# Recording only the second of two exponentials as user of a PSUM group, where the group spans two pairs' buffers

## The chip, the cores and the metric

The kernel runs on one core of one Trainium2 chip. The time is device time in microseconds of one execution, and the median of several runs is given. A profile of one execution was taken with the hardware profiler; its span runs from the first instruction to the last.

## What is computed

Queries are averaged two by two, scored against all keys, passed through a softmax and applied to the values. The result, put back in token order, goes through a layer with a maximum of two projections and an output projection.

```python
q_pool = q.reshape(B, H, S // 2, 2, D).mean(axis=3)      # B 8, H 8, S 1152, D 64
scores = np.matmul(q_pool, k.transpose(0, 1, 3, 2)) / np.sqrt(D)
attn = softmax(scores)                                   # over the keys
x = np.matmul(attn, v).transpose(0, 2, 1, 3).reshape(B * S // 2, H * D)   # 4608 x 512
out = np.maximum(x @ w1, x @ w2) @ w_out                 # 512 -> 1024 -> 512
```

## The kernel before

The 64 heads are worked on as 32 pairs of heads. For a pair, POOL adds neighbouring queries (qp) and casts keys (kbf) and values (vE). The queries are transposed to qpT: by PE for the first five pairs, and from pair 5 on (`Q_PE = 5`) by eight 32-row transposes on DVE, `qtrans_dve` at L378, where the eighth (n = 7) alone is recorded as the writer of qpT. The keys are transposed to kT by PE for the first pairs and by a DMA later.

The scores of all pairs form one long row of columns, 5184 (`PW`) for each pair, and this row is cut into 324 groups of 512 columns (`W`). For a group, PE computes the scores of both heads into one of the PSUM tiles sps (L515), and ACT takes the exponential of both heads' 512 columns (L522, 128 x 1024 elements) into the SBUF tile et. Three sps tiles take turns at first; from the point `turn_at` on there are two, and the third serves other matmuls. et has room for two pairs (one of each parity), so its columns wrap after every second pair, that is every 10368 columns. Every fourth such wrap falls on a group's edge; at the other 12 the group is split, and ACT runs two exponentials, one up to `turn` and one from it. They are 256 and 768, 512 and 512, or 768 and 256 elements of a partition, in rotation.

When a pair's exponentials are done, PE multiplies them with the values (L425 and L437, called attention-times-V here) into a bank of fb or of the third sps tile, and DVE divides by the sums (L447 to L457). Blocks of the later layers fill PE in between: L727 makes the hidden values, DVE applies the ReLU (L736), L760 makes the output, DVE copies it out of PSUM (L771). When the scores are all done, the rest of these blocks follows (L700 and L793).

The order on each engine is not written by hand. A planner (`Plan`) records every operation with the keys that it reads and writes, and a scheduler picks PE's next unit by planned times. `deps` makes an operation depend on the last writer of each key that it reads or writes, and on the readers of each key that it writes; only the former, for keys that it reads, are kept as raw dependencies. `solve` turns dependencies into semaphore waits. A dependency on an operation of the same engine is left out by this line (L102), unless it is a raw one on an engine other than PE:

```python
if p["eng"] == eng and not o["fence"] and (eng == "PE" or eng != "DVE" and d not in o["raw"]):
    continue
```

A wait is also left out where the engine has already waited for a later operation of the same engine. Each exponential reads the key s{r} of its sps tile and writes it too, so that the next scores into that tile wait for it. Where a group is split, both halves do so.

Of the kernel before, what the change touches and what calls it, by code (L numbers as in the profile page):

```python
# [16 lines left out]
class Plan:  # L17
# [40 lines left out]
    def op(self, eng, fn, r=(), w=(), dma=None, cost=0.1, mode="f", after=(), solo=False,  # L58
           fence=False):
        n = len(self.ops)  # L60
        assert all(k in self.writer for k in r), r
        deps, raw = self.deps(r, w, after)
        prev = self.last.get(eng)
        if prev is not None and (solo or self.ops[prev]["solo"]):
            deps.add(prev)
            raw.add(prev)
        self.last[eng] = n
        t = self.when(eng, r, w, after, fence)
        if dma is not None:
            if not self.dma_free:  # L70
                t = 0.78
            self.free[eng] = t + (1.3 if mode == "t" else 0.5)
            a = max(self.free[eng] + 1.2, self.dma_free)
            self.dma_free = a + cost + (1.9 if a < 5.0 <= a + cost else 0.0)
            seen = self.dma_free + 0.7
        else:
            if eng == "PE" and mode != self.mode:
                t += 0.1
                self.mode = mode
            self.free[eng] = t + cost  # L80
            seen = t + cost + self.LAT[eng]
        self.ops.append(dict(eng=eng, fn=fn, deps=deps, raw=raw, dma=dma, w=tuple(w),
                             seen=seen, end=self.free[eng], solo=solo, fence=fence))
        for k in r:
            self.readers.setdefault(k, set()).add(n)
        for k in w:
            self.writer[k] = n
            self.readers[k] = set()
        return n
# [72 lines left out]
def bass_funnel_attn__then__act_maxout2_kernel(  # L162
# [32 lines left out]
    with ctx:  # L195
        def sbuf(shape, dt, name):
            return ctx.enter_context(nc.sbuf_tensor(name, list(shape), dt))
# [9 lines left out]
        qp = [t[0:HP, :, :, :] for t in qpw]  # L207
        qpf = [t.rearrange("p u h d -> p (u h d)")[:, 0:QU * D].rearrange("p (u d) -> p u d", d=D)
               for t in qpw]
        qpT = [sbuf([P, SQ], BF16, f"qpT{s}") for s in range(3)]  # L210
        kbf = [sbuf([P, NT, 2, D], BF16, f"kbf{s}") for s in range(2)]
        kT = [sbuf([P, NT, P], BF16, f"kT{s}") for s in range(3)]
# [27 lines left out]
        def rows(half):  # L240
            return slice(half * HP, half * HP + HP)

        Q0 = (0, 4, QU)
        QA = 4 * HP
# [127 lines left out]
        def qtrans_dve(i, n):  # L372
            s, z = i % 2, i % 3
            h, pb, db = n // 4, n // 2 % 2, n % 2
            src, dst = 64 * h + 32 * pb, 64 * h + 32 * db
            view = qpT[z][:, :].rearrange("p (u x) -> p u x", x=HP)
            last = [f"qpT{z}"] + (["qpT0.0"] if i == 3 else []) if n == 7 else []
            op("DVE", lambda e: e.transpose(  # L378
                view[dst:dst + 32, :, 32 * pb:32 * pb + 32],
                qpf[s][src:src + 32, :, 32 * db:32 * db + 32]),  # L380
                r=[f"qp{s}.0", f"qp{s}.1"], w=last, after=[f"qpT{z}"] + (["qpT0.0"] if i == 3 else []), cost=0.37)
            if n == 7:
                q_done.add(i)

# [81 lines left out]
        def first(i):  # L466

            return i * PW // W
# [15 lines left out]
        def pieces(g):  # L484

            a = g * W
            while a < (g + 1) * W:
                i = a // PW
                x = a - i * PW
                for c, z in runs(i):  # L490
                    if x < NT * (z - c):
                        break
                    x -= NT * (z - c)
                t, lo = x // (z - c), c + x % (z - c)
                n = min((g + 1) * W - a, z - lo)
                yield i, t, lo, lo + n, a - g * W
                a += n

        def pairs_of(g):
            return sorted({i for i, *_ in pieces(g)})  # L500

        def skeys(g):
            return [key for i, t, lo, *_ in pieces(g) for key in (
                f"kT{i % 3}.{t}", "qpT0.0" if i == 0 and lo < QA else f"qpT{i % 3}")]

        def ring(g):
            return g % 3 if g < turn_at[0] else (g - turn_at[0]) % 2

        def scores(g):
            r = ring(g)  # L510

            def pe(e):
                for i, t, lo, hi, col in pieces(g):
                    for h in range(2):
                        last = e.matmul(  # L515
                            sps[r][:, h, col:col + hi - lo], kT[i % 3][rows(h), t, :],
                            qpT[i % 3][rows(h), lo:hi], start=True, stop=True)
                return last

            def exp(a, z, keys):  # L520
                c = a % (2 * PW)
                op("ACT", lambda e: e.activation(  # L522
                    et2[:, :, c:c + z - a], sps[r][:, :, a - g * W:z - g * W], EXP, scale=scale),
                    r=[f"s{r}"], w=keys + [f"s{r}"], cost=0.05 + (z - a) / 600.0)

            op("PE", pe, r=skeys(g), w=[f"s{r}"], cost=PE_S, mode="s")
            a, z = g * W, (g + 1) * W
            turn = z // (2 * PW) * 2 * PW
            keys = {i: [f"et{i % 2}.{g - first(i)}"] for i in pairs_of(g)}
            if a < turn < z:  # L530
                i = turn // PW
                exp(a, turn, keys[i - 1])
                exp(turn, z, keys[i])
            else:
                exp(a, z, sum(keys.values(), []))
# [331 lines left out]
        Q_PE = 5  # L867
# [72 lines left out]
        def flush():  # L940
# [21 lines left out]
            if turns and plan.free.get("DVE", 0.0) <= now():  # L962
                qtrans_dve(*turns.pop(0))
# [75 lines left out]
        def banks(job, kk):  # L1039
            if job.single:  # L1040
                return [f"f{kk}", f"f{kk + 1}"]
            return [f"f{kk + (len(job.units[0]) > 4)}"]
# [23 lines left out]
        def burst_now(size):  # L1066

            todo_g = range(nxt, min(nxt + size, NGR))
            if not todo_g:
                return None, 0.0  # L1070
            for g in todo_g:
                for p, t, *_ in pieces(g):
                    if (any(key not in plan.writer for key in skeys(g)) if p == 0 else p not in q_done) or k_hi.get(p, 0) <= t or (
                            p >= 2 and av_half.get(p - 2) != 2):
                        return None, 0.0
            t = now() + 0.1
            stall = 0.0
            for g in todo_g:
                s = plan.when("PE", r=skeys(g), w=[f"s{ring(g)}"])
                stall += max(0.0, s - t)  # L1080
                t = max(t, s) + PE_S
            return todo_g, stall

        def emit_burst(todo_g):
            nonlocal nxt, entered
            for g in todo_g:
                while entered < pairs_of(g)[-1]:
                    entered += 1
                    enter(entered)
                scores(g)  # L1090
                for p in pairs_of(g):
                    if g == after(p) - 1:
                        queue["a"].extend(av_jobs(p))
            nxt += len(todo_g)
            if nxt == NGR:
                more_banks((0, 1) if turn_at[0] < NGR else (0, 1, 2))
                for kind in "hp":
                    queue[kind] = [j for job in queue[kind] for j in (job.single() if job.single else [job])]
            if queue["q"]:
                for kk in (0, 1):  # L1100
                    if lane.get(kk, 0) is None and plan.when(
                            "PE", r=queue["q"][0].units[0][0], w=[f"f{kk}"]) <= now() + 0.05:
                        lane[kk] = queue["q"].pop(0)
                        emit_unit(kk)
                        break
# [81 lines left out]
        while p_end[0] < NTOK:  # L1187
# [14 lines left out]
            for kk in lane:  # L1202
                job = lane[kk]
                if job is not None:
                    t = plan.when("PE", r=job.units[0][0], w=banks(job, kk), fence=len(job.units[0]) > 4 and job.units[0][4] == 2)
                    cand.append((t, -rank[job.kind], len(job.units), kk))
            fresh = [c for c in cand if c[0] <= now() + 0.03]
            turn = [c for c in fresh if lane[c[3]].units[0][3] == "c"]
# [97 lines left out]
```

## Time and profile before

| | us |
|---|---|
| median of 4 runs | 378.97 |
| lowest and highest | 378.62, 380.17 |
| the profiled execution | 379.0 |
| its span | 377.2 |
| PE, ACT, DVE, POOL busy | 360.2, 316.2, 238.2, 124.9 |
| mean of an exponential with 1024, 768, 512, 256 elements of a partition | 1.048, 0.834, 0.614, 0.414 |

The granted clock of PE is 1.0 over the whole execution. The mean of an exponential is the length of its record; records of neighbouring exponentials can overlap, so that lengths do not add up to time, and ends or starts have to be compared. A busy PE is not PE at its peak, for its matmuls are pipelined and their ends are modelled.

### The profile page before, as it was taken

The page shows a single profiled execution, that of the slowest core. Times are in us where ns is not written, and L with a number is a line of the kernel's source. Part 1 is how long each engine was busy: PE and PEld are TensorE (multiplying, and loading weights), DVE is VectorE, ACT ScalarE, POOL GpSimd, SP SyncE. Part 2 cuts the span into 40 slices and gives each one's busy share as a digit, 9 for nine tenths or more (in the row PEclk, how much of TensorE's full clock was granted, in tenths as well). Part 3 has the DMA queues.
Part 4 walks back from the last instruction along what each step waited for, and adds up shares of the span by engine and source line. Part 5 has one row for each costly group of instructions (what it writes and reads, how often), then busy time and mean ns, then how long its engine had stood idle before and what let it go on. Part 6 is the DMA issues. An engine that isn't in the chain of part 4 may idle for free.

```text
span 377.2 us, 12691 instructions
## 1 busy us (share of the span) xinstructions
PE 360.2 (95%) x5613; PEld 202.8 (54%) x5621; DVE 238.2 (63%) x516; ACT 316.2 (84%) x360; POOL 124.9 (33%) x111
## 2 busy tenths in 40 slices
PE   4899999999999999999999999999999999999996
PEld 1464556555555464554555555555556554665463
DVE  2685499966677667765686668866786635342231
ACT  4999799999999999999999999999999999811131
POOL 1359965362324333333333333432333010000000
PEclk9999999999999999999999999999999999999999
DMA  8999999999999799989799989979996451012324
GB/s 297 404 395 400 398 275 323 329 260 307 166 302 303 233 227 235 276 249 235 198 306 276 258 168 335 298 212 94 266 286 115 86 94 32 2 29 59 82 57 111
DMA packets 76823, 84.68 MB, mean 224 GB/s; under 512 B 49376, under 2 KB 49632, under 8 KB 76768
## 3 DMA queue, kind: packets, MB, share of 16 engines
q1 hardware_dynamic: 75888, 82.56, 81.0%
q10 hardware_dynamic: 880, 1.31, 0.9%
q8 instruction: 44, 0.72, 0.9%
q14 instruction: 11, 0.09, 0.1%
HBM read 62.91 MB, written 9.44 MB: 192 GB/s over the span
## 4 chain that ended last, share of the span: by engine, by line
PE 60%; ACT 28%; DVE 8%; issue 1%; DMA 1%; SPq 0%
ACT et L522 28%; PE sps L515 14%; PE sps L425 9%; PE sps L760 8%; PE fb L425 7%; PE sps L793 5%; DVE qpT L378 5%; PE fb L760 3%; PE sps L727 2%; PE fb L727 2%; PE sps L700 2%; PE fb L700 2%; PE sps L437 1%; PE fb L793 1%; PE fb L437 1%
## 5 line engine op out<-in xcount | busy, mean ns | idle before, releaser
L522 ACT ACTIVATE et<-sps 128x1024 bf16<-128x1024 f32 (+1 forms) x336 | 305.1, 1018 | 17.2 <-PE sps L515 15.4
L515 PE MATMUL sps<-qpT,kT 64*128 64x256 bf16 (+7 forms) x1162 | 120.5, 290 | 6.1 <-ACT et L522 2.3
L378 DVE STREAM_TRANSPOSE qpT<-qp 32x288 bf16<-32x288 bf16 x216 | 101.3, 469 | 34.1 <-PE sps L515 22.5
L324 POOL TENSOR_SCALAR vE<-vraw 128x1152 bf16<-128x1152 f32 x32 | 36.9, 1154 | 150.9 <-PE sps L425 92.0
L515 PEld LDWEIGHTS sps<-qpT,kT 64*128 64x128 bf16 x1162 | 39.4, 94 | 83.8 <-ACT et L522 67.7
L318 POOL TENSOR_TENSOR qp<-qraw 128x576 bf16<-128x576 f32 x30 | 42.1, 1405 | 13.1 <-DMA qraw<-in_q_dram 7.9
L425 PE MATMUL fb<-vE,et 128*128 128x65 bf16 x1152 | 40.7, 193 | 0.0
L425 PE MATMUL sps<-vE,et 128*128 128x65 bf16 x1152 | 40.4, 193 | 0.0
L425 PEld LDWEIGHTS fb<-vE,et 128*128 128x128 bf16 x1152 | 36.7, 97 | 4.7 <-issue 3.7
L425 PEld LDWEIGHTS sps<-vE,et 128*128 128x128 bf16 x1152 | 36.5, 97 | 4.1 <-issue 3.5
L285 POOL TENSOR_SCALAR kbf<-kraw 128x1152 bf16<-128x1152 f32 x31 | 35.7, 1153 | 8.5 <-DMA kraw<-in_k_dram 6.3
L727 PE MATMUL fb<-xT,wd 64*128 64x512 bf16 (+1 forms) x240 | 35.9, 373 | 0.3
L727 PE MATMUL sps<-xT,wd 64*128 64x512 bf16 x224 | 33.0, 376 | 0.0
L760 PE MATMUL sps<-wo,stage 64*128 64x512 bf16 x224 | 31.9, 376 | 0.0
L760 PE MATMUL fb<-wo,stage 64*128 64x512 bf16 x192 | 27.6, 376 | 0.0
L736 DVE TENSOR_SCALAR stage<-fb 128x1024 bf16<-128x1024 f32 (+1 forms) x15 | 18.1, 1205 | 11.2 <-PE fb L727 11.1
L736 DVE TENSOR_SCALAR stage<-sps 128x1024 bf16<-128x1024 f32 x14 | 17.1, 1220 | 12.6 <-PE sps L727 12.3
L760 PE MATMUL sps<-w,xT 64*128 64x512 bf16 x112 | 16.6, 378 | 0.8 <-DVE xnat L457 0.6
L727 PEld LDWEIGHTS fb<-xT,wd 64*128 64x128 bf16 x240 | 11.2, 94 | 10.0 <-PE fb L727 2.1
L771 DVE COPY stage<-sps 128x1024 f32<-128x1024 f32 x7 | 8.6, 1224 | 12.3 <-PE sps L760 12.3
L793 PE MATMUL sps<-wo,stage 128*128 128x512 bf16 (+2 forms) x71 | 15.6, 355 | 0.0
L760 PEld LDWEIGHTS sps<-wo,stage 64*128 64x128 bf16 x224 | 10.7, 94 | 8.3 <-issue 0.4
(68 smaller groups left out, 276.9 us busy)
## 6 DMA issues: line engine op xcount, KB each, us to landing
kraw<-in_k_dram SPq DMA_DIRECT2D x32, 576.0 KB, 7.1
vraw<-in_v_dram SPq DMA_DIRECT2D x32, 576.0 KB, 8.1
qraw<-in_q_dram SPq DMA_DIRECT2D x31, 576.0 KB, 6.5
out_dram<-stage SPq DMA_DIRECT2D x19, 256.0 KB, 4.4
out_dram<-stage SPq DMA_DIRECT2D x23, 128.0 KB, 2.7
xT<-in_moe_w_dram SPq DMA_DIRECT2D x4, 512.0 KB, 10.0
stage<-in_moe_w_out_dram SPq DMA_DIRECT2D x4, 512.0 KB, 13.8
stage<-in_moe_w_dram SPq DMA_DIRECT2D x4, 512.0 KB, 14.0
```

The costliest lines, as they stand in the source:

```text
L285: op("POOL", lambda g: g.tensor_scalar(kbf[s][:, :, :, :].rearrange("p t h d -> p h t d"), kraw[r][:, :, :, :], 1.0, 1.0, ALU.mult, ALU.mu ...
L318: op("POOL", lambda g: g.tensor_tensor(qpf[s][:, :, :], qraw[r][:, :, 0, :], qraw[r][:, :, 1, :], ALU.add), r=[f"qraw{r}"], w=[f"qp{s}.0", ...
L324: op("POOL", lambda g: g.tensor_scalar(vE[r][:, :, :, 0:D].rearrange("p t h d -> p h t d"), vraw[r][:, :, :, :], 1.0, 1.0, ALU.mult, ALU.m ...
L378: op("DVE", lambda e: e.transpose(view[dst:dst + 32, :, 32 * pb:32 * pb + 32], qpf[s][src:src + 32, :, 32 * db:32 * db + 32]), r=[f"qp{s}. ...
L425: last = e.matmul(fb[m][:, sb * 66:sb * 66 + 65], et[:, a:a + P], vE[vs][:, t, half, 0:65], start=(t == 0), stop=(t == NT - 1))
L515: last = e.matmul(sps[r][:, h, col:col + hi - lo], kT[i % 3][rows(h), t, :], qpT[i % 3][rows(h), lo:hi], start=True, stop=True)
L522: op("ACT", lambda e: e.activation(et2[:, :, c:c + z - a], sps[r][:, :, a - g * W:z - g * W], EXP, scale=scale), r=[f"s{r}"], w=keys + [f" ...
L700: return e.matmul(fb[m][:, 0:size], wd[:, ct, ft * P:(ft + 1) * P], xT[:, ct, n0:n1], start=(ct == 0), stop=(ct == NC_ - 1))
L727: last = e.matmul(fb[m + k][:, 0:size], wd[z, ct, (f0 + k) * P:(f0 + k + 1) * P], xT[z, ct, n0:n1], start=(turn == 0 and ct == 0), stop=(t ...
L736: dve(lambda e: e.tensor_scalar_max(gT[:, f0:f0 + 2, g0:g0 + size], wide[m // 2][:, :, 0:size], 0.0), [f"f{m}", f"f{m + 1}"], w + [f"f{m}" ...
L760: last = e.matmul(fb[m + k][:, :], lhs, rhs, start=(turn == 0 and j == 0), stop=(turn == 1 and j == NC_ + NF - 1))
L793: return e.matmul(fb[m][:, 0:c1 - c0], lhs, rhs[:, c0:c1], start=(j == 0), stop=(j == NC_ + NF - 1))
```

## The change

Where a group is split, the first exponential no longer writes the key s{r}; it still reads it and still writes its own key of et. In addition each of the eight query transposes of a pair on DVE writes a key of its own, qt{z}.{n}, and the scores of a group read all eight keys of every pair from 5 on that the group touches.

```diff
-                r=[f"qp{s}.0", f"qp{s}.1"], w=last, after=[f"qpT{z}"] + (["qpT0.0"] if i == 3 else []), cost=0.37)
+                r=[f"qp{s}.0", f"qp{s}.1"], w=[f"qt{z}.{n}"] + last, after=[f"qpT{z}"] + (["qpT0.0"] if i == 3 else []), cost=0.37)
...
         def skeys(g):
             return [key for i, t, lo, *_ in pieces(g) for key in (
-                f"kT{i % 3}.{t}", "qpT0.0" if i == 0 and lo < QA else f"qpT{i % 3}")]
+                f"kT{i % 3}.{t}", "qpT0.0" if i == 0 and lo < QA else f"qpT{i % 3}")] + [
+                f"qt{i % 3}.{n}" for i in pairs_of(g) if i >= Q_PE for n in range(8)]
...
-            def exp(a, z, keys):
+            def exp(a, z, keys, last=True):
                 c = a % (2 * PW)
                 op("ACT", lambda e: e.activation(
                     et2[:, :, c:c + z - a], sps[r][:, :, a - g * W:z - g * W], EXP, scale=scale),
-                    r=[f"s{r}"], w=keys + [f"s{r}"], cost=0.05 + (z - a) / 600.0)
+                    r=[f"s{r}"], w=keys + ([f"s{r}"] if last else []), cost=0.05 + (z - a) / 600.0)
...
             if a < turn < z:
                 i = turn // PW
-                exp(a, turn, keys[i - 1])
+                exp(a, turn, keys[i - 1], False)
                 exp(turn, z, keys[i])
```

## The prediction

> **What bounds the kernel now.** I read the page first, then the waits by engine, then the windows by stage, then single instructions on ACT, PEld and DVE around the split groups, and last the chain of waits.
>
> The busy shares alone do not decide it: PE is busy 95% of the span, ACT 84%. The waits say more.
>
> ```profile
> PE 360.2 (95%) x5613; PEld 202.8 (54%) x5621; DVE 238.2 (63%) x516; ACT 316.2 (84%) x360; POOL 124.9 (33%) x111
> ...
> PEld sps L515 <- ACT et L522: 67.7, 183, 1.0
> ACT et L522 <- PE sps L515: 15.4, 38, 2.5
> ...
> 103.00:110.00 7.00, 6.74 (x82) 2.50 (x78) 5.18 (x9) 6.97 (x9) 3.03 (x3) 1.00 0.95 312
> 203.00:207.90 4.90, 4.89 (x56) 2.32 (x56) 2.20 (x4) 4.87 (x7) 2.68 (x3) 1.00 0.69 254
> ```
>
> A score group's weight load waits 183 times for an exponential (the two-buffer or three-buffer sps ring), while ACT waits 38 times for scores. So up to about 327 us the exponentials set the pace inside a stretch, and PE sets it where a block of attention-times-V matmuls comes between. The two window rows (columns: length, then PE, PEld, DVE, ACT, POOL) show both kinds: from 103 to 110 us ACT is full (6.97 of 7.00) and PE has 0.26 us to spare; from 203 to 207.9 us PE itself is full (4.89 of 4.90). After 327 us there is no exponential left and PE alone runs to the end.
>
> **The change, part by part.** There are 324 groups and 336 exponentials, so 12 groups are split in two. The built programs have the same instructions in the same order on all five engines. What differs is on ACT alone: in all 12 splits the second half no longer waits for ACT's own semaphore, and in nine of them the first half no longer increments it (later waits count accordingly). The new keys qt z.n and their 8 reads in skeys add no wait: the eight transposes of a pair run in order on DVE, and PE already waits for the eighth. I cost the keys and the nine dropped increments at nothing; there is no instruction behind either, nothing is moved past a queue, and no wait is added, so nothing new can queue behind one.
>
> What the dropped wait costs is read on ACT. These are rows of the timeline in narrow windows (start, length, count; a row of two covers the named instruction and the next one):
>
> ```profile
> 106.27 1.05 ACT L522 ACTIVATE et<-sps 128x1024 bf16<-128x1024 f32 x1
> 106.27 1.33 ACT L522 ACTIVATE et<-sps 128x1024 bf16<-128x1024 f32 x2
> 107.18 1.27 ACT L522 ACTIVATE et<-sps 128x256 bf16<-128x256 f32 x2
> 107.64 1.72 ACT L522 ACTIVATE et<-sps 128x768 bf16<-128x768 f32 x2
> ...
> 146.11 1.05 ACT L522 ACTIVATE et<-sps 128x1024 bf16<-128x1024 f32 x1
> 146.11 1.76 ACT L522 ACTIVATE et<-sps 128x1024 bf16<-128x1024 f32 x2
> 147.01 1.27 ACT L522 ACTIVATE et<-sps 128x768 bf16<-128x768 f32 x2
> ```
>
> At 107 us the last whole group ends at 106.27 + 1.05 = 107.32, the first half (256 columns) at 106.27 + 1.33 = 107.60, the second (768) at 107.18 + 1.27 = 108.45. So 256 columns cost 0.28 us where they follow without a self-wait, and 768 cost 0.85 with it. At 147 us the sizes are the other way round: 768 without the wait takes 147.87 - 147.16 = 0.71, 256 with it 148.28 - 147.87 = 0.41. Like against like the wait costs 0.85 - 0.71 = 0.14 and 0.41 - 0.28 = 0.13 us; I take 0.14. In the starts it looks larger: the second half begins at 107.64, 0.03 after the first half's end, while without a wait the first half began at 107.18, 0.14 before its forerunner's end, which makes 0.17 to 0.18. I use the ends, because PE's next score is released by an end.
>
> Two rules of the Trainium skill can be set against this row. In "VectorE: DVE Perf Modes", section "The DRAIN you can't avoid", eight VectorE copies take the same time with a semaphore after each as with one after the last: the semaphore costs nothing extra. Carried over to ACT, the change would be worth 0 and the time 378.97. The rows above speak against carrying it over: on this engine neighbours overlap and a self-wait ends the overlap. "ScalarE: Activation LUTs", section "What ACT_TABLE_LOAD costs", says that back-to-back ACTIVATEs overlap by about 93 ns; with the 0.03 us gap that is 0.12 us a split instead of 0.14, by estimate. I keep the 0.14 measured here as the value and hold 0 and 0.18 as the ends.
>
> Now which of the 12 lie on the path. PE must be waiting for that very end, and nothing else may hold PE just after it. Weight loads at these places (bracket: idle before, and who ended it), and the DVE rows that answer two of them:
>
> ```profile
> 107.38 0.11 PEld L515 LDWEIGHTS sps<-qpT,kT 64*128 64x128 bf16 x4 [0.37 <-ACT et L522]
> 108.50 0.11 PEld L515 LDWEIGHTS sps<-qpT,kT 64*128 64x128 bf16 x4 [0.57 <-ACT et L522]
> ...
> 71.01 0.17 PEld L437 LDWEIGHTS sps<-vE,et 128*64 128x64 bf16 x6 [0.21 <-DVE stage L736]
> 129.88 0.24 PEld L437 LDWEIGHTS fb<-vE,et 128*64 128x64 bf16 x10 [0.43 <-DVE stage L771]
> ...
> 69.73 1.17 DVE L736 TENSOR_SCALAR stage<-sps 128x1024 bf16<-128x1024 f32 x1
> 128.60 1.23 DVE L771 COPY stage<-fb 128x1024 f32<-128x1024 f32 x1
> ...
> by line: DVE qpT L378 59.1%; DVE xnat L457 17.0%; DVE xnat L452 9.1%; DVE rc L447 7.5%; DVE w L643 6.0%; issue 4.0%; PE fb L425 0.7%
> ```
>
> - Splits at 26, 107, 147, 187, 227, 267 and 308 us: the score after the second half is released 0.05 after its end (108.45 to 108.50) and PEld has idled 0.57 (0.54 at 26), against 0.37 at the ordinary group before. There are 0.2 us to win, more than 0.14. The next block of attention-times-V also needs DVE to have emptied its bank: at 107 that was done at 109.26 for a block at 109.74, at 187 it was done 0.75 earlier, at 267 0.47, at 147, 227 and 308 about 0.27, and at 26 no such hold follows. A wait takes at least 0.05, so 0.22 is to spare. Seven times 0.14 = 0.98 us.
> - Split at 67 us: the block at 71.01 needs DVE's ReLU, which ends at 69.73 + 1.17 = 70.90. DVE has run without a gap since 66 us, so an earlier ACT does not make it earlier. Only 71.01 - 70.90 - 0.05 = 0.06 us can be won.
> - Split at 127 us: the block at 129.88 is released by DVE's copy, which ends at 129.83. DVE works off transposes from 126.7 to 128.6 before it. Worth 0.
> - Split at 47.5 us: the chain in the window 46 to 56 us is DVE work, 59% of it the qpT transposes. Worth 0.
> - Splits at 207 and 287 us: PE is full (second window row) and the chain runs through its matmuls. Worth 0.
>
> Sum: 0.98 + 0.06 = 1.04 us. What PE gains it keeps: each new ACT stretch starts by waiting for PE, DVE's later runs start by waiting for PE, and the tail from 327 us is PE. Against the profiled execution (379.0 us, span 377.2 and 1.8 around it) that gives 377.96; against the median of the runs, 378.97, it gives 377.9.
>
> **The rivals.**
> *More than that (chance 0.17).* If the overlap is worth the 0.18 of the starts and the DVE hold at 67 and 127 us gives way, nine sites bring 9 x 0.18 = 1.6; all twelve at 0.14 bring 1.7. Time 377.3. For it: the gap of 0.03 and the overlap are both real. Against it: PE is released by ends, and DVE rows at 70.90 and 129.83 stand where they stand.
> *Hidden (chance 0.20).* PE is 95% busy, and if the 0.2 us of idle at a split is taken up by PE's own spacing or by a DVE evacuation just after, the gain is 0 to 0.4. Time 378.8. For it: three sites are hidden already for such reasons, and spare times of 0.22 us are small. Against it: the 0.57 against 0.37 repeats at six of the seven sites, and the seventh has 0.54.
> *Slower (chance 0.08).* The place is the load queue: the stretch from 92 to 328 us has the DMA engines busy 87% of the time by the windows view. PE earlier by 0.1 to 1 us frees q, k and kT buffers earlier, so SP issues earlier, and a kT transpose can fall into a load. It took 2.8 us to land at best, 4.8 in the median, 9.8 at worst. It decides once a landing comes after the score that needs it; today no wait of PE for a DMA appears among the 60 longest waits. One such landing, 9.8 instead of 4.8, of which I assume 3 us hidden, would cost 2 us, less the gain of 1.0: 380.0.
> That the change does nothing at all is excluded by the program: the 12 waits are gone.
>
> **How the numbers follow.** Main case 0.55 at 377.9, with 377.5 to 378.3 for its own spread; more 0.17 at 377.3; hidden 0.20 at 378.8; slower 0.08 at 380.0. A measurement of this kernel can tell about 0.3%, or 1.1 us, from no change (the runs before lie within 378.62 to 380.17). The line for faster is thus 377.83, and the main case lies just short of it: I give it 0.4 to come out below and 0.6 within. Faster: 0.55 x 0.4 + 0.17 x 0.95 = 0.38. Same: 0.55 x 0.6 + 0.2 + a little = 0.54. Slower: 0.08. The range 377.1 to 378.7 holds the main case, most of the larger gain and half of the hidden one.
>
> **What would show it right or wrong.** In the profile after, the second half of a split should start about 0.15 before the first half's end, and the two halves should end 0.99 us after the group before them, not 1.13. PEld's idle before the score after a split should fall from 0.57 to about 0.43. The block after 127 us should idle longer for DVE by what ACT gained, and the score waits at 207 and 287 us should not change. ACT's last exponential should end about 1.0 us earlier. A gain over 1.4 us, or PE waits for ACT at 207 us, would make my list of sites wrong; halves that still do not overlap would make the price wrong; a PE wait for kT's DMA would be the slower rival.

## The result, and the profile after

The changed kernel took 378.38 us in the median (38 runs, 377.42 to 381.36), against 379.0 us for the kernel before beside it (59 runs, 378.51 to 381.53). The ratio is 0.9985, with a 95% interval of 0.9975 to 0.9996. The profiled execution took 377.75 us, with a span of 376.0.

The page of the kernel after, its span and busy times:

```profile
span 376.0 us, 12691 instructions
...
PE 359.5 (96%) x5613; PEld 202.6 (54%) x5621; DVE 238.3 (63%) x516; ACT 314.9 (84%) x360; POOL 124.9 (33%) x111
```

The span is 1.2 us shorter, and every engine ran as many instructions as before. Lines from 505 on are numbered one higher than before (L522 is now L523). The splits at 107 and 147 us, from the timeline of ACT after the change, in narrow windows (start, length, count):

```profile
105.83 1.05 ACT L523 ACTIVATE et<-sps 128x1024 bf16<-128x1024 f32 x1
106.73 0.43 ACT L523 ACTIVATE et<-sps 128x256 bf16<-128x256 f32 x1
106.99 0.87 ACT L523 ACTIVATE et<-sps 128x768 bf16<-128x768 f32 x1
...
145.59 1.05 ACT L523 ACTIVATE et<-sps 128x1024 bf16<-128x1024 f32 x1
146.49 0.85 ACT L523 ACTIVATE et<-sps 128x768 bf16<-128x768 f32 x1
147.19 0.44 ACT L523 ACTIVATE et<-sps 128x256 bf16<-128x256 f32 x1
```

At 107 us the second half now begins at 106.99, which is 0.17 before the first ends (106.73 + 0.43 = 107.16); before, it began 0.03 after that end. The two halves end 106.99 + 0.87 - (105.83 + 1.05) = 0.98 after the whole group ahead of them; before it was 1.13. At 147 us it is 147.63 - 146.64 = 0.99. PE's weight loads of the scores around 107 us, and of the block behind the split at 127 us (bracket: idle before, and who ended it):

```profile
106.93 0.11 PEld L516 LDWEIGHTS sps<-qpT,kT 64*128 64x128 bf16 x4 [0.37 <-ACT et L523]
107.91 0.11 PEld L516 LDWEIGHTS sps<-qpT,kT 64*128 64x128 bf16 x4 [0.43 <-ACT et L523]
...
129.36 0.36 PEld L437 LDWEIGHTS fb<-vE,et 128*64 128x64 bf16 x18 [0.56 <-DVE stage L772]
```

The score behind the split idles 0.43 where it idled 0.57. The block after 127 us idles 0.56 where it idled 0.43: what ACT won is spent waiting for DVE. The waits by engine (total, times, longest) have fallen by 1.4 us for scores on exponentials, and the reverse wait has grown by 0.3:

```profile
PEld sps L516 <- ACT et L523: 66.3, 187, 0.8
ACT et L523 <- PE sps L516: 15.7, 37, 2.5
```

The best view for the question which split keeps its gain is the timeline of ACT over a longer window: it joins neighbouring exponentials into one row as long as ACT does not stand still, and the bracket of the next row says how long ACT then waited. First the kernel before, around 47.5, 67, 127, 147 and 207 us:

```profile
47.50 13.14 ACT L522 ACTIVATE et<-sps 128x512 bf16<-128x512 f32 x15 [2.51 <-PE sps L515]
61.17 1.02 ACT L522 ACTIVATE et<-sps 128x1024 bf16<-128x1024 f32 x1 [0.52 <-PE sps L515]
...
63.90 8.57 ACT L522 ACTIVATE et<-sps 128x1024 bf16<-128x1024 f32 x10
72.78 3.03 ACT L522 ACTIVATE et<-sps 128x1024 bf16<-128x1024 f32 x3 [0.30 <-PE sps L515]
...
123.27 7.63 ACT L522 ACTIVATE et<-sps 128x1024 bf16<-128x1024 f32 x9
131.36 1.02 ACT L522 ACTIVATE et<-sps 128x1024 bf16<-128x1024 f32 x1 [0.47 <-PE sps L515]
...
141.39 10.56 ACT L522 ACTIVATE et<-sps 128x1024 bf16<-128x1024 f32 x12
152.25 1.02 ACT L522 ACTIVATE et<-sps 128x1024 bf16<-128x1024 f32 x1 [0.30 <-PE sps L515]
...
201.23 7.80 ACT L522 ACTIVATE et<-sps 128x1024 bf16<-128x1024 f32 x9
209.39 1.02 ACT L522 ACTIVATE et<-sps 128x1024 bf16<-128x1024 f32 x1 [0.36 <-PE sps L515]
```

The same runs of exponentials after the change:

```profile
47.28 13.00 ACT L523 ACTIVATE et<-sps 128x512 bf16<-128x512 f32 x15 [2.52 <-PE sps L516]
60.78 1.94 ACT L523 ACTIVATE et<-sps 128x1024 bf16<-128x1024 f32 x2 [0.50 <-PE sps L516]
...
63.51 8.44 ACT L523 ACTIVATE et<-sps 128x1024 bf16<-128x1024 f32 x10
72.33 3.03 ACT L523 ACTIVATE et<-sps 128x1024 bf16<-128x1024 f32 x3 [0.38 <-PE sps L516]
...
122.75 7.50 ACT L523 ACTIVATE et<-sps 128x1024 bf16<-128x1024 f32 x9
130.85 1.02 ACT L523 ACTIVATE et<-sps 128x1024 bf16<-128x1024 f32 x1 [0.60 <-PE sps L516]
...
140.87 10.42 ACT L523 ACTIVATE et<-sps 128x1024 bf16<-128x1024 f32 x12
151.60 1.94 ACT L523 ACTIVATE et<-sps 128x1024 bf16<-128x1024 f32 x2 [0.30 <-PE sps L516]
...
200.43 7.67 ACT L523 ACTIVATE et<-sps 128x1024 bf16<-128x1024 f32 x9
208.58 1.02 ACT L523 ACTIVATE et<-sps 128x1024 bf16<-128x1024 f32 x1 [0.49 <-PE sps L516]
```

Every one of the five runs is 0.13 or 0.14 us shorter, so the price is the same everywhere. What differs is the wait that follows. At 147 us it is 0.30 both times: the gain is kept. At 127 and 207 us it grows by 0.13: the gain is given back whole. At 67 us it grows by 0.08: about half is kept. At 47.5 us it does not grow (0.52 before, 0.50 after), so most of the gain is kept, which the prediction had not expected. The kernel before is itself 0.05 us late at this place in the trace shown: other traces in which the wait stands there read 0.47 or 0.48, and beside them the wait has grown by 0.02 or 0.03.

### The profile page after: what moved, and what is told of

It reads as the page before. It is cut to its first block, busy times and chain, and to the rows that moved or that the text cites. A ratio compares the mean times of both kernels' runs of the same rounds, so it can differ in the third digit from the quotient of the medians.

```text
span 376.0 us, 12691 instructions
## 1 busy us (share of the span) xinstructions
PE 359.5 (96%) x5613; PEld 202.6 (54%) x5621; DVE 238.3 (63%) x516; ACT 314.9 (84%) x360; POOL 124.9 (33%) x111
## 4 chain that ended last, share of the span: by engine, by line
PE 67%; ACT 20%; DVE 9%; issue 1%; DMA 1%; SPq 0%; DVEq 0%
ACT et L523 20%; PE sps L516 15%; PE sps L425 9%; PE sps L761 8%; PE fb L425 7%; PE sps L794 5%; DVE qpT L378 5%; PE fb L761 5%; PE fb L728 4%; PE sps L728 4%; PE sps L701 2%; PE fb L701 2%; PE sps L437 2%; PE fb L794 1%; PE fb L437 1%
## 5 line engine op out<-in xcount | busy, mean ns | idle before, releaser
L523 ACT ACTIVATE et<-sps 128x1024 bf16<-128x1024 f32 (+1 forms) x336 | 303.8, 1033 | 17.1 <-PE sps L516 15.7
L772 DVE COPY stage<-sps 128x1024 f32<-128x1024 f32 x7 | 8.6, 1223 | 12.3 <-PE sps L761 12.3
```

What stands on the lines that cost most here:

```text
L523: op("ACT", lambda e: e.activation(et2[:, :, c:c + z - a], sps[r][:, :, a - g * W:z - g * W], EXP, scale=scale), r=[f"s{r}"], w=keys + ([f ...
```

## The experiments

To compare two traces split by split, the starts of PE's 5621 weight loads, which stand in the same order in both, were subtracted one by one. A split's gain below is what this difference has lost, by medians, from the loads just ahead of the split to the loads behind the last step that belongs to it, so that what is given back is taken off (us; the sums are those of the unrounded values):

| split at | 26 | 47.5 | 67 | 107 | 127 | 147 | 187 | 207 | 227 | 267 | 287 | 308 | sum |
|---|---|---|---|---|---|---|---|---|---|---|---|---|---|
| predicted | .14 | 0 | .06 | .14 | 0 | .14 | .14 | 0 | .14 | .14 | 0 | .14 | 1.04 |
| changed | .14 | .11 | .06 | .14 | 0 | .14 | .14 | .01 | .14 | .14 | 0 | .14 | 1.14 |
| changed, third time | .14 | .11 | .05 | .14 | 0 | .14 | .14 | -.01 | .13 | .14 | 0 | .14 | 1.12 |
| seven splits alone | .14 | 0 | 0 | .14 | 0 | .13 | .14 | 0 | .14 | .14 | 0 | .14 | .96 |
| three splits alone | 0 | 0 | 0 | 0 | 0 | 0 | 0 | 0 | 0 | 0 | 0 | 0 | 0 |

Steps that belong to no split are not in the table: loads that land earlier or later in the first 29 us, stalls of PE without a wait, and a step of -0.05 at 60.4 us, which every trace shows, that of *before_again* too, because the kernel before was late there in the trace that the others are compared with. In the profile after the change these steps come to about -0.08 us in all, in the others to between 0 and +3.2.

**The two parts of the change, and both kernels once more.** The change has two edits, and they can be made apart. *exp_only* has the exponentials' edit alone, *qt_only* the query transposes' keys alone:

```diff
 exp_only
-                exp(a, turn, keys[i - 1])
+                exp(a, turn, keys[i - 1], False)
 qt_only
-                r=[f"qp{s}.0", f"qp{s}.1"], w=last, ...
+                r=[f"qp{s}.0", f"qp{s}.1"], w=[f"qt{z}.{n}"] + last, ...
```

Beside them ran the kernel before (*before_again*) and the changed kernel (*after_again*), unedited.

> Only the half of the change that concerns the exponentials; no keys for the eight query transposes. Theory A: the same as the changed kernel, ratio 0.997 to 0.9985, the same steps of 0.14 us in the profile. Rival C (the new keys cost or gain something): a ratio that differs from the changed kernel's by more than 0.001.

> Only the keys for the eight query transposes; both halves of a split write the group's key as before. Theory A: the program has no other wait than before, ratio 1.000, no step in the profile at the splits. Rival C: a ratio away from 1 by more than 0.001.

> The kernel before, against itself. Both theories: ratio 1.000. The distance from 1 shows what a ratio of this many runs is worth, and a second profile of it shows how far two profiles of one program differ: I expect steps of 0.1 to 0.3 us in the first 20 us, where the loads land, and few later.

> The changed kernel, unchanged, in five more rounds beside the kernel before. Theory A (nine of the twelve dropped waits lie on the path, 0.14 us each, two of them partly given back): ratio 0.997 to 0.9975, and in the profile the last exponential ends about 1.1 us earlier than before. Theory B (most executions give half of it back in a wait that a single profile does not show): ratio about 0.9985, and a profile in which steps of 0.14 us are lost again at some later instruction.

| | median us | runs | ratio to before | 95% interval |
|---|---|---|---|---|
| before, beside them | 379.27 | 67 | | |
| exp_only | 378.38 | 22 | 0.9982 | 0.9966 to 0.9999 |
| qt_only | 379.62 | 22 | 1.0007 | 0.9992 to 1.0022 |
| before_again | 378.9 | 14 | 0.9999 | 0.9982 to 1.0016 |
| after_again | 378.4 | 22 | 0.998 | 0.9965 to 0.9995 |

The split at 107 us in exp_only and then in qt_only, from the timeline of ACT (one row for both halves):

```profile
106.46 1.13 ACT L522 ACTIVATE et<-sps 128x256 bf16<-128x256 f32 x2
...
107.07 1.27 ACT L523 ACTIVATE et<-sps 128x256 bf16<-128x256 f32 x2
```

The two halves take 1.13 with the exponentials' edit and 1.27, as before the change, with the keys alone. The keys do nothing. In the traces, the splits sum to 1.13 us in exp_only and to 1.11 in after_again, and in qt_only no step stands at any split. The exponentials' edit drops 12 waits and nine increments of ACT's semaphore. At 26, 207 and 287 us the first half still increments it, by the trace after the change, and there the second half ends 0.138 to 0.139 us earlier, as at the nine others: so it is the wait that counts, and the increment costs nothing that shows. The ratio of after_again, 0.998, lies between what the two theories forecast and does not decide; in the traces no step is lost again but at the places named above.

**The price by itself.** In both of the next kernels all 312 groups that lie in one pair's buffer are cut in two as well, into halves of 256 columns of each head. In *halves_wait* the first half writes s{r}, so that the second waits for ACT; in *halves_free* it does not, and the 12 splits are treated in the same way. Nothing else differs: the order of the instructions on PE, DVE, ACT and POOL is the same in both traces. (`whole` is the planner's cost of an uncut group.)

```diff
-                exp(a, z, sum(keys.values(), []))
+                exp(a, a + W // 2, sum(keys.values(), []), True, whole / 2)    # halves_free: False
+                exp(a + W // 2, z, sum(keys.values(), []), True, whole / 2)
```

> Every whole group is here two exponentials of 256 columns of each head (128 x 512 elements) instead of one of 128 x 1024, and the first writes s{r} too, so that each second half waits for ACT's own semaphore. My theory (a self-wait ends the overlap of neighbours and costs 0.14 us at the end of the second half) expects halves to end about 0.55 us apart where the second waited against about 0.41 where it did not, no overlap of the second's start with the first's end, and, over about 300 groups paced by ACT for most of the time, 30 to 42 us more than the version without these waits. A theory in which the wait itself costs nothing and the gain at the splits comes from elsewhere expects the two versions within 1 us of each other.

> The same halves as in the run beside it, but the first half does not write s{r}, so that no second half waits for ACT itself. My theory expects the two halves together to take about 2 x 0.49 us or less, the second starting 0.1 us or more before the first's end, and a time some 10 to 25 us over the changed kernel, for what an instruction costs besides its columns (0.28 us for 256, 0.71 for 768, so about 0.065 fixed). The free-wait theory expects the same time as with the waits.

halves_wait took 427.92 us (ratio 1.1287, 1.1263 to 1.1311, 2 runs), halves_free 392.47 us (1.0352, 1.0329 to 1.0375, 2 runs). The first row is ACT's timeline in halves_wait, the second in halves_free, three groups each; below them, in the same order, the wait of scores for exponentials:

```profile
125.01 3.45 ACT L523 ACTIVATE et<-sps 128x512 bf16<-128x512 f32 x6
...
112.43 3.18 ACT L523 ACTIVATE et<-sps 128x512 bf16<-128x512 f32 x6
```

```profile
PEld sps L516 <- ACT et L523: 129.4, 246, 1.0
...
PEld sps L516 <- ACT et L523: 91.8, 232, 0.9
```

In halves_wait the ends follow each other by 0.488 and, where the second half waited, by 0.628: 0.14 us for the wait, at a size (128 x 512) at which the prediction had not measured it. The expectation had the difference right and both steps 0.08 too short (0.41 and 0.55). In halves_free both steps are 0.49. The row's length, from the first start to the last end, differs by less than three waits because the last record is longer where records overlap (0.791 against 0.597). Over the whole kernel the difference is 427.92 - 392.47 = 35.5 us, for 312 + 12 = 324 waits, or 0.110 for each. A part of it is not the wait: PE came to its full clock at 25.4 us in halves_wait and at 14.3 in halves_free (see the last section). From the 31st group on, when both had it, ACT's ends move apart by 31.7 us over 294 groups, 0.108 for each, which is 77% of 0.14. That would fit three quarters of the groups being paced by ACT and the rest having the wait hidden; it was not counted group by group. That the wait costs nothing is refuted. What an additional exponential costs without a wait is 0.98 - 0.917 = 0.063 us a group in the ends, and (392.47 - 378.38) / 312 = 0.045 in the time.

**Which splits count.** The edit is made at some splits and not at others, by the number of the group g:

```diff
-                exp(a, turn, keys[i - 1], False)
+                exp(a, turn, keys[i - 1], g not in (20, 101, 141, 182, 222, 263, 303))   # sites_seven
+                exp(a, turn, keys[i - 1], g not in (121, 202, 283))                      # sites_hidden
```

> The first half is left out as a writer of s{r} at the splits of 26, 107, 147, 187, 227, 267 and 308 us alone; the other five keep the wait. The prediction's site list expects the whole gain but 0.06 us: in the trace about 0.98 us less at the last exponential, apart from stalls that are no waits, 377.9 to 378.1 in the median. If the split at 47.5 us holds its part as the trace of the changed kernel suggests, this version is 0.14 to 0.16 us behind the changed kernel. A theory by which the gain is not the sum of the sites (a few sites carry it all, or a chance shift of the stream) expects anything else.

> The first half is left out as a writer of s{r} only at the splits of 127, 207 and 287 us, where the prediction says that DVE or PE takes the gain back. It expects each second half to end 0.14 us earlier and the next score or block to be where it was: last exponential within 0.05 us of before apart from stalls that are no waits, ratio 1.000. A theory in which all splits count the same expects 3 x 0.14 = 0.42 us less (ratio 0.9989).

> The kernel with the wait dropped only at 127, 207 and 287 us once more, unchanged. Its first run had a ratio of 1.002 though its trace showed no lost step at any split, but a stall of 2.2 us at 20.7 us and one of 1.3 us at 192.6 us. If these are chance of one loading of the program, the ratio now is 1.000 within 0.001. If they belong to this program (its size or its place in memory), the ratio is 1.002 again and the stalls are at the same places.

sites_seven: 378.69 us, ratio 0.9994 (0.9976 to 1.0013, 14 runs). sites_hidden: 380.35 us, ratio 1.002 (1.0003 to 1.0036, 18 runs), and the second time 379.18 us, ratio 1.0003 (0.999 to 1.0016, 14 runs). The times of these two cannot settle a tenth of a microsecond; the traces can. The seven splits bring 0.96 us, of 0.98 predicted (table), and 0.18 less than the changed kernel's 1.14, where 0.14 to 0.16 was expected. The three bring 0: at 127 us the score comes 0.139 earlier and the block behind it 0.140 later, in both traces alike, and at 207 and 287 us no weight load moves. The run of exponentials at 47.5 us in sites_seven, where the wait stays:

```profile
47.38 13.14 ACT L523 ACTIVATE et<-sps 128x512 bf16<-128x512 f32 x15 [2.51 <-PE sps L516]
```

It has the old length, 13.14, and no step follows. So the 0.11 us of the changed kernel at this place is the dropped wait, not chance. The ratio of 1.002 did not come again, and the dropped waits are not its cause: the first profiled execution had lost 1.9 us by 29 us and 1.3 us in a stall at 192 us, of which the last section tells. The second had no stall at 192 us, but it too had lost 1.4 us by 29 us, as no other trace of this group size had. Whether that loss belongs to this program is open, and so is whether it or the chip made the first ratio: the two ran on different chips.

**The hold of DVE at 127 us.** Here the changed kernel's planner is kept from issuing query transposes while group 122 or 123 is the next, so that four of them come behind DVE's copy L772 instead of ahead of it. The order on PE, ACT, POOL and SP stays.

```diff
-            if turns and plan.free.get("DVE", 0.0) <= now():
+            if turns and plan.free.get("DVE", 0.0) <= now() and nxt not in (122, 123):
```

> The changed kernel, and beside it four of the eight query transposes on DVE are put behind DVE's copy L771 (here L772) at 128.6 us, so that the copy comes about 1.5 us earlier; order on PE, ACT, POOL and SP as before. The prediction says that the split at 127 us brought nothing because the block at 129.88 waits for that copy. It expects the block now to keep the 0.14 us that ACT gained there, and up to 0.1 us more, for the block idled 0.43 of which about 0.2 was DVE's hold: in the trace 0.14 to 0.25 us less than the changed kernel from 130 us on, apart from stalls that are no waits. A rival, that PE or ACT itself is the limit at 129.9 us, expects no step there against the changed kernel. Another, that the transposes put off are late for the scores of the next pair, expects a new wait of PE for DVE's L378 and a time up to 1 us longer.

> The changed kernel once more, as it is, beside the others on the same chip. Expected: 12 splits with a second half ending 0.14 us earlier, of which 9 keep it (8 whole, that at 67 us in part): about 1.1 us less in undisturbed executions, 0.6 to 0.9 less in the median, since stalls of up to 1 us that are no waits fall into many executions of both kernels.

hold took 378.01 us (ratio 0.9968, 0.9956 to 0.998, 22 runs), the changed kernel beside it 377.92 us (0.996, 0.9948 to 0.9972, 12 runs): the two cannot be told apart by their times. In the trace of hold, the DVE copy, PE's block, and the run of exponentials with the wait behind it:

```profile
127.84 1.23 DVE L772 COPY stage<-fb 128x1024 f32<-128x1024 f32 x1 [4.29 <-PE fb L761]
...
129.41 0.36 PEld L437 LDWEIGHTS fb<-vE,et 128*64 128x64 bf16 x18 [0.42 <-DVE stage L772]
...
122.94 7.50 ACT L523 ACTIVATE et<-sps 128x1024 bf16<-128x1024 f32 x9
130.90 1.02 ACT L523 ACTIVATE et<-sps 128x1024 bf16<-128x1024 f32 x1 [0.46 <-PE sps L516]
```

The copy now ends at 129.07, 0.34 before the block, where in the kernel before it ended 0.05 before it. The run is as short as in the changed kernel (7.50), and the wait behind it is back at 0.46, from 0.60. So the split at 127 us keeps its 0.14 us (the splits of hold sum to 1.27), and DVE was what took it. No more than that came: the block follows its score by 129.41 - 128.65 = 0.76 us, exactly as in the kernel before (129.88 - 129.12), where the copy ended at the same instant. What else sets these 0.76 us is not shown; that it is PE's own spacing is only argued. The profile still names DVE's copy as the releaser, though the copy had ended 0.34 earlier. No late transpose showed as a new wait.

## Why the prediction was right or wrong

*The price.* It was read as 0.14 us from ends at two splits. At all 12 splits the second half ends 0.138 to 0.140 earlier after the change, against the group ahead of it, and the 312 waits between halves of another size give 0.14. The value from the starts, 0.17 to 0.18, did not show in any end.

*The rules weighed against it.* The Trainium skill's "VectorE: DVE Perf Modes", section "The DRAIN you can't avoid", carried over to ACT, would have given 0; the page speaks of VectorE only. The 93 ns of "ScalarE: Activation LUTs", section "What ACT_TABLE_LOAD costs", gave 0.12 by the prediction's estimate. The runs agree with the measured row: 0.14. By that estimate the seven splits would have summed to 0.84; sites_seven has 0.96.

*The list of splits.* The seven full splits, the zero at 127, 207 and 287 us and the part at 67 us (0.06 predicted, 0.05 to 0.06 measured) came out. (One reading was too neat: the idle of 0.37 us at the group ahead of a split is only 0.28 or 0.29 at 147, 187 and 267 us. It changes nothing, as the 0.57 at the split is the same.) The step "Split at 47.5 us: the chain in the window 46 to 56 us is DVE work ... Worth 0" failed: it brought 0.10 to 0.11. DVE does hold PE in that stretch, at 52.8 and at 55.9 us, and each time PE's difference goes back by 0.14. But the next score waits for ACT again, and ACT had not stood still: it ran 15 exponentials in a row from 47.5 to 60.6 us. As long as ACT has work in store, a hold of PE by DVE is a pause of PE, not of the engine that sets the pace. The chain says who was last at each step inside its window; it does not say that an earlier ACT is lost there. At 127 us the hold of DVE was long enough to let ACT run dry (0.47 of idle before, 0.60 after), and that makes the difference.

*The size.* The sum was 1.04; the splits measured 1.11 to 1.14 in four traces, the difference being the split at 47.5 us. ACT's last exponential ended at 326.29 + 1.95 = 328.24 before and at 325.97 + 1.04 = 327.01 after, 1.23 earlier, of which about 0.08 belongs to no split. The forecast of 377.9 for the median was nevertheless 0.5 too low beside the 378.38 of the first comparison. Over the changed kernel's three sets (72 runs) against all runs of the kernel before beside the experiments (198 runs), the medians are 378.3 and 379.14: 0.83 us apart, with a 95% interval of 0.47 to 1.17 by resampling, and the lowest runs 0.99 apart. That contains both the predicted 1.04 and the traced 1.1. The three comparisons taken one by one gave 0.62, 0.87 and 1.33. So whether the 0.62 of the first is a real shortfall is not settled: both kernels have executions that lose 1 us and more at places that no split touches, and a median over them is no clean measure of 1 us.

*The rivals.* "More" asked for the overlap of 0.18 or for the hold at 67 and 127 us to give way; neither happened. "Hidden" happened at three splits, which the main case had already at 0. "Slower" by a late kT transpose did not show: no wait of PE for a DMA is among the 60 longest waits after the change either.

## What to carry to other kernels

Where an engine paces the kernel, look for waits of this engine for itself: between two exponentials on ACT one such wait cost 0.14 us, and here it was not needed, because both halves only read the PSUM tile and the second already carries the dependency of the next scores. To find out whether a gain on the pacing engine is kept, look at its next standstill in the timeline: if the run of instructions gets shorter and the wait behind it does not grow, the gain is kept, and a hold of another engine in between, as at 47.5 us, has not taken it. And when a difference is well below the spread of the runs, compare the starts of the same instructions in two traces, step by step, and use the times only as a check on the sum. Take a second trace of the unchanged kernel as well: it shows which steps belong to the first trace alone, as that of 0.05 us at 60.4 us here.

## What the runs showed of the hardware that was not expected

**PE's speed-up comes at another time in some executions.** Twenty-seven weight loads of attention-times-V at about 19 us, first in the kernel before, then in sites_hidden:

```profile
18.29 0.36 PEld L437 LDWEIGHTS fb<-vE,et 128*64 128x64 bf16 x18 [0.21 <-issue]
18.70 0.87 PEld L425 LDWEIGHTS fb<-vE,et 128*128 128x128 bf16 x27
...
19.06 0.57 PEld L437 LDWEIGHTS fb<-vE,et 128*64 128x64 bf16 x18 [0.41 <-issue]
19.70 1.50 PEld L425 LDWEIGHTS fb<-vE,et 128*128 128x128 bf16 x27
```

The same 27 loads take 0.87 or 1.50 us. The rows of the profile give the granted clock as 1.00 for this stretch in both, but there it means only that nothing is recorded: in the packed trace, the record of the clock begins with an entry of full clock at 16.3 us in the kernel before and at 23.2 us in sites_hidden. (The clock of 1.0 over the whole execution, given for the kernel before, is thus recorded only from 16.3 us on.) In all thirteen traces the weight loads change at this entry: their mean record is 125 to 138 ns in the 8 us ahead of it, and 98 to 100 ns behind it. The entry comes at 13.4 to 16.3 us in nine of the eleven profiles at full group size, and at 23.2 and 22.0 us in the two of sites_hidden, which are 1.9 and 1.4 us behind the kernel before at 29 us.

The Trainium skill, "TensorE: Matmul & The Clock Gate", section "Part 1: The HAM clock gate", describes such a change of clock, decided in a free-running window of 3413 ns, and says that its moment varies from run to run with the place of that window. The traces agree with the window: the full-clock entry lasts 358.40, 361.81 or 365.23 us in these eleven, in steps of 3.41. Its place alone does not explain the late entries: they come 6.9 us after that of the kernel before and 6.8 us after that of the changed kernel, two whole steps, so that each pair shares nearly the same place. In both late traces the query average L311 had released PE 0.25 to 0.34 us later than before at 14.5 us; but in the changed kernel's trace it was 0.24 later too, and the entry came at 15.2 us. What delays it is open.

**Stalls of PE without a wait, at fixed places.** At about 192 us a weight load comes without delay in one execution and up to 1.5 us late in another, of which up to 1.3 stays, with no semaphore to wait for ("issue"). The timeline of PEld in the kernel before, then in qt_only, where the fourth of the same loads comes late:

```profile
192.12 0.11 PEld L515 LDWEIGHTS sps<-qpT,kT 64*128 64x128 bf16 x4
...
192.44 0.11 PEld L516 LDWEIGHTS sps<-qpT,kT 64*128 64x128 bf16 x3
193.65 0.09 PEld L516 LDWEIGHTS sps<-qpT,kT 64*128 64x128 bf16 x1 [1.10 <-issue]
```

It is the same instruction of PE's stream in every kernel here, and so is a second place at 116.4 us (up to 0.6). The packed traces also hold the DMA packets, among them 44 of 16 KB of the kind "instruction" on queue q8. The last one ahead of the load at 192 us ended at 188.7 us in the kernel before and at 192.3 in qt_only. In the six of the eleven traces in which the load is late, it starts 1.2 to 1.5 us after that packet's end (1.35 in qt_only); in the five in which it is not late, the packet had ended 1.25 to 5.3 us before. At 116.4 us it is alike: 1.4 to 1.6 us in the four late traces, 1.6 to 2.1 in the others. So a late fetch of instructions fits every trace. It is not shown by an experiment, for none moved the fetch, and why it comes late in some executions is open.

**Records of exponentials grow while their ends keep time.** Within an undisturbed run of whole groups the ends are 917 ns apart and the starts 904, so that each record overlaps the next by 13 ns more than the one ahead of it did. The mean record of a whole group rose from 1048 to 1063 ns with the change, while the kernel became faster. Lengths of records are no measure of ACT here; ends are.
